# Round 0's second outputs before round 1's transposes, and a closing slot of round 1 without conversions begun: a fused RWKV-6 and MLP kernel

## The chip, the cores and the metric

The kernel runs on one core of a Trainium2 chip. The metric is the device time of one execution in microseconds, the median of several runs. Before the change it is 594.73 us (four runs: 592.81, 593.84, 595.62, 599.49). The run of 595.62 us is the one that was profiled; its span is 593.6 us.

The engines are named as in the profile: PE (TensorE matmul), PEld (its weight load), DVE (VectorE), ACT (ScalarE), POOL (GpSimd), SP (SyncE, which issues most of the DMAs here). Each engine takes its instructions in order, and an instruction that waits holds up all those behind it on its engine.

## The reference

Two stages in float32. The first is a linear attention with a state per head (batch 4, 8 heads, 768 steps, head dimension 48):

```python
for t in range(S):
    kt, vt, rt, wt = (k[:, :, t], v[:, :, t], r[:, :, t], w[:, :, t])
    cur = np.einsum('bhd,bhe->bhde', u[None] * kt, vt)
    y[:, :, t] = np.einsum('bhd,bhde->bhe', rt, state + cur)
    state = wt[:, :, :, None] * state + np.einsum('bhd,bhe->bhde', kt, vt)
```

Its output, as 4 x 768 x 384, goes through a normalised MLP with a residual:

```python
mu = np.mean(x, axis=-1, keepdims=True)
var = np.mean((x - mu) ** 2, axis=-1, keepdims=True)
xn = (x - mu) / np.sqrt(var + 1e-06) * g_ln
ch = np.maximum(xn @ w_ch1, 0.0) @ w_ch2
return (x + ch).astype(np.float32)
```

## The kernel before

The work is cut into eight rounds (four batches by two halves of 384 steps), and each round into two units of four heads. Units are numbered on: round 0 has units 0 and 1 (`u0`, `u1`), round 1 has 2 and 3 (`new[0]`, `new[1]` in the opening), and so on.

For a unit, `turned` transposes w, k and r with PE into PSUM (`w_ps`, `k_ps`, `r_ps`) and ACT copies the result to SBUF (`wT`, `rkT`). The part of the output that comes from inside a chunk of 64 steps is built in six levels: `quads` makes small matmuls into `a_ps`, `grow` multiplies r and k by products of decays on DVE, and `keep` moves the masked result from `a_ps` into `A`. `totals` makes the products of decays (`tot`, `decay`) for a round. At the end of a round `ends` transposes k (`kn_ps`, copied by ACT to `kn`), `finish` copies what is left of A and r, `states` multiplies k and v into `kv` and walks the state over the chunks on DVE (`s`), `exchanged` copies half of it across partitions on ACT (`sx`). `own_outputs` and `outputs` put the result together in PSUM (`y`), and DVE adds the term of u (`vo`, from `own_term` on POOL) to give `x`. That term needs `product_sums`, which multiplies the products r times k (`ruk`, from `products`) by u on PE, and a copy by ACT to `own`.

Then the MLP of the round: `moments` (statistics on DVE), `norm` (a root on ACT, `rstd`, then a reciprocal and three scalings on DVE, `xn`), `turned_x` (PE into `xT_ps`, ACT to `xT`), and `mlp`, a generator. One step of it is three matmuls and, in its first half, the ReLU on ACT: twelve steps make `h` from `h_ps`, and the later ones make `o_ps`. The matmuls of the MLP fill PE between the small stages of the attention part. They use two PSUM buffers in turn (`ps_m`), so a step needs the ReLU of two steps before it. Transposes use two others (`ps_t`), and `a_ps`, `kv` and `y` two more (`ps_a`).

The MLP weights are 24 parts of 128 x 384. They come in as raw words and are converted once, in rounds 0 and 1. For a part, `begin` makes three activations on ACT (a `w_sb` and two of `held` or `rest`) and issues the fetch of the part four further on; `join` is `shifted` (two DVE instructions) and `added` (one). From part 12 on, the rest goes into four buffers in turn, so `begin` of a part needs the join of the part four before it. A part must be joined before the MLP step that reads it.

The order on each engine is that of the program text for everything recorded through the wrapped engines (`PE`, `ACT`, `DVE`, `POOL`, `SPO`); loads through the plain `SP` are placed by the scheduler. The opening (lines 697 to 776) writes the order out by hand. From round 1 on the slots (round, level) are filled by `fill`, which spreads a list of tasks over the MLP steps that the slot gets (`UNTIL`); `mixed` interleaves lists by their relative place. In round 1 each slot adds begins and joins by two tables:

```python
JOINS, BEGINS = (3, 3, 3, 4, 4, 4), (3, 3, 3, 3, 4, 2)
```

The last slot of round 1 (level 5) is called the closing slot here. `warm` issues matmuls on zeros (`idle` in the profile); three columns of 128 make one matmul, two rows in the profile.

Of the kernel before, what the change touches and what calls it, by code (L numbers as in the profile page):

```python
# [52 lines left out]
def kernel(  # L53
# [31 lines left out]
    NLEV = 6  # L85
# [181 lines left out]
    def join():  # L267
        shifted()
        added()
# [89 lines left out]
    def product_sums(q):  # L359
        b, f, g = units[q]  # L360
        a = st[q]
        ps = ps_t.tile([P, RN], F32, tag="t", name=f"own_ps{q}")
        for pr in pairs:
            for c in range(TT):
                PE.matmul(
                    ps[:, ts(pr * TT + c, 2)], a["ruk"][pr][:, ts(c, P)],
                    sel[:, NP * g + pr], start=True, stop=True,
                )
        o = a["own"] = p4.tile([P, TT, NH], F32, tag="own", name=f"own{q}")
        ACT.copy(  # L370
            out=o.rearrange("p c (r j) -> p r c j", j=2),
            in_=ps[:, 0 : 2 * NK].rearrange("p (r c j) -> p r c j", r=NP, j=2),
        )

    def own_term(q, eng):
        a = st[q]
        a["vo"] = p4.tile([P, TT, NH, D], F32, tag="vo", name=f"vo{q}")
        eng.tensor_tensor(
            out=a["vo"], in0=vn[q],
            in1=a["own"][:, :, :, None].broadcast_to([P, TT, NH, D]), op=ALU.mult,  # L380
        )
# [117 lines left out]
    def exchanged(q):  # L499

        a = st[q]
        a["sx"] = p2.tile([P, NP, TT, D], F32, tag="sx", name=f"sx{q}")
        for j in range(2):
            ACT.copy(
                out=a["sx"][ds(HP * (1 - j), HP)],
                in_=a["s"].rearrange("p r (c i) e -> p r c i e", i=2)[ds(HP * j, HP), :, :, 0],
            )
# [3 lines left out]
    def own_outputs(q, tag="a"):  # L511

        y = ys[q] = banks(tag, f"y{q}")
        A = a_bufs[q // U % 2]
        for k_ in range(NK):
            pr, c = divmod(k_, TT)
            for i in range(2):
                for j in range(2):
                    rows = ds(C * (i ^ j), C)
                    PE.matmul(  # L520
                        y[j][ds(C * i, C), k_], A[rows, j, q % U, k_, :],
                        vx[q][rows, c, pr] if j else vn[q][rows, c, 2 * pr],
                        start=k_ == 0, stop=False, skip_group_check=True,
                    )
# [157 lines left out]
    def run(tasks):  # L682
        for t in tasks:
            t()

    def units_of(rnd):
        return [U * rnd + g for g in range(U)] if rnd < NR else []
# [37 lines left out]
    ahead = each(turned, new[:1], "wrk", pairs) + each(turned, new[1:], "wrk", pairs)  # L725
# [22 lines left out]
    exchanged(u0)  # L748
    states(u1)
    product_sums(u1)  # L750
    own_term(u1, POOL)
    own_outputs(u0)
    warm(3, "t")
    outputs(u0)
    exchanged(u1)
    own_outputs(u1, "m")
    warm(3, "t")
    run(ahead[8:])
    quads(new[0], 0)
    join()  # L760
    outputs(u1)
    load(units_of(2)[0], "w", SPO)
    load(units_of(2)[1], "w", SPO)
    products(new[1], POOL)
    begin()
    moments(0)
    shifted()
    quads(new[1], 0)
    product_sums(new[0])
    warm(6)  # L770
    norm(0)
    added()
    begin()
    join()
    run(each(turned_x, [0], range(KC)))
    mlps.append(mlp(0))

# [5 lines left out]
    while len(UNTIL) < NR * NLEV:  # L783
        UNTIL.append(UNTIL[-1] + MLP_STEPS // NLEV)
    ahead = [t for nm in "wkr" for t in each(turned, units_of(2), nm, pairs)]
    JOINS, BEGINS = (3, 3, 3, 4, 4, 4), (3, 3, 3, 3, 4, 2)
    for rnd in range(1, NR + 1):
        old, now, new = units_of(rnd - 1), units_of(rnd), units_of(rnd + 1)
        if rnd == 1:
            old = []  # L790
        for lev in range(NLEV):
            slot = (rnd - 1) * NLEV + lev
            if rnd == 2:

                for q in old if lev < 2 else []:
                    (states, outputs)[lev](q)
                if lev < 2:
                    mlp_step()
            elif old and lev < 2 * U:
                (states if lev < U else outputs)(old[lev % U])  # L800
            for q in now:
                if slot:
                    quads(q, lev)
            for which in ("rk",) if lev < NLEV - 1 else "kr":
                for q in now:
                    grow(q, lev, which)
            if now:
                if rnd == 1 and lev == 0:
                    totals(rnd, DVE)
                keep(rnd, lev)  # L810
            tasks = []
            if rnd == 1:
                if lev < 2:
                    tasks += each(load, new, "kr"[lev], [SPO])
                if lev == 2:
                    SPO.dma_start(
                        out=u_bc,
                        in_=bass.AP(
                            tensor=u.tensor, offset=u.offset, ap=[[0, P], [D, H], [1, D]]
                        ),  # L820
                    )
                    tasks += each(load_v, now, [SPO])
                if lev == 3:
                    tasks += each(load_vx, now, [SPO])
                if lev == 1:
                    tasks += each(product_sums, now[1:])
                if lev in (4, 5):
                    own_term(now[lev - 4], POOL)
            if rnd == 2 and lev == 0:
                tasks += each(load_v, now) + each(load, new, "w")  # L830
            if rnd == 2 and lev == 2:
                for q in now:
                    take(DVE, q)
                    tasks += each(load, new[q % U :][:1], "kr")
            if rnd == 2 and lev in (3, 4):
                tasks += each(own_term, now[lev - 3 :][:1], [POOL])
            if rnd > 2 and lev < 2:
                tasks += each(load, new, ["w", "kr"][lev])
            first = 3 if rnd == 2 else 1
            if rnd > 1 and new and first <= lev < first + 3:  # L840
                m = lev - first
                tasks += each(turned, new[m - 1 : m], "kr", pairs) if m else each(
                    turned, new, "w", pairs
                )
            if rnd == 2:
                if lev == 0:
                    tasks += each(exchanged, old)
                if lev == 1:
                    tasks += [lambda: moments(1), lambda: norm(1)]
                if lev == 2:  # L850
                    tasks += each(turned_x, [1], range(KC))
            elif old and lev < U:
                tasks += each(exchanged, [old[lev]])
            if lev == 3 and rnd > 1:
                for q in now:
                    load_vx(q)
                for q in new:
                    load_v(q)
                if rnd > 2:
                    moments(rnd - 1)  # L860
                    tasks += each(norm, [rnd - 1])
            if lev == 4 and rnd > 2:
                tasks += each(turned_x, [rnd - 1], range(KC))
                tasks += each(own_products, new[:1], [POOL])
            if lev == NLEV - 1:

                if now:
                    mlp_step()
                if rnd > 2 and new:
                    own_sums(new[0])  # L870
                if rnd == 2:
                    tasks += each(own_products, new[:1], [POOL]) + each(own_sums, new[:1])
                if rnd >= 2:
                    tasks += each(own_term, new[:1], [POOL])
                    tasks += each(own_products, new[1:], [POOL])
                    tasks += each(own_sums, new[1:]) + each(own_term, new[1:], [POOL])
                if new:
                    tasks += each(totals, [rnd + 1], [POOL])
                if now:
                    tasks = mixed(  # L880
                        tasks,
                        each(ends, now, pairs) + each(finish, [2, 2, 4])
                    )
            if rnd == 1:

                n = (1, 2, 2, 1, 0, 0)[lev] * NP
                tasks += mixed([begin] * BEGINS[lev], [join] * JOINS[lev], ahead[:n])
                del ahead[:n]
            fill(UNTIL[slot], tasks)
            if lev == (2 if rnd == 2 else 4) and old:  # L890
                mlps.append(mlp(rnd - 1))
# [32 lines left out]
```

## Time and profile before

| | |
|---|---|
| median of four runs | 594.73 us |
| profiled run | 595.62 us, span 593.6 us |
| PE busy | 571.2 us, 96% |
| PEld busy | 383.3 us, 65% |
| DVE busy | 279.1 us, 47% |
| ACT busy | 195.4 us, 33% |
| POOL busy | 93.8 us, 16% |
| mean granted PE clock | 0.989 |

The busy shares are means over stages that differ. The span in 40 slices of 14.8 us (a digit is a tenth; PEclk is the granted clock in tenths of full speed) shows where they differ:

```profile
PE   8999998799999999899999999999999999999997
DVE  4877998668365444425255334426245431130000
ACT  3557786303352125211243114321241015301200
PEclk9989999799999999989999999999999999999999
```

Slices 0 to 2 hold the load and round 0. In slices 4 and 5 (59 to 89 us) DVE and ACT are as busy as PE, with the conversion of the weights beside round 1. Slice 7 (104 to 119 us) is the end of round 1 and the start of round 2. From there on DVE and ACT have slack, and PE is busy nearly throughout.

### The profile page before, as it was taken

The page shows a single profiled execution, that of the slowest core. Times are in us where ns is not written, and L with a number is a line of the kernel's source. Part 1 is how long each engine was busy: PE and PEld are TensorE (multiplying, and loading weights), DVE is VectorE, ACT ScalarE, POOL GpSimd, SP SyncE. Part 2 cuts the span into 40 slices and gives each one's busy share as a digit, 9 for nine tenths or more (in the row PEclk, how much of TensorE's full clock was granted, in tenths as well). Part 3 has the DMA queues.
Part 4 walks back from the last instruction along what each step waited for, and adds up shares of the span by engine and source line. Part 5 has one row for each costly group of instructions (what it writes and reads, how often), then busy time and mean ns, then how long its engine had stood idle before and what let it go on. Part 6 is the DMA issues. An engine that isn't in the chain of part 4 may idle for free.

```text
span 593.6 us, 19016 instructions
## 1 busy us (share of the span) xinstructions
PE 571.2 (96%) x8540; PEld 383.3 (65%) x8540; DVE 279.1 (47%) x574; ACT 195.4 (33%) x426; POOL 93.8 (16%) x118
## 2 busy tenths in 40 slices
PE   8999998799999999899999999999999999999997
PEld 5776765466666666666666666667666665666554
DVE  4877998668365444425255334426245431130000
ACT  3557786303352125211243114321241015301200
POOL 6041022004260026000250006100240000000000
PEclk9989999799999999989999999999999999999999
DMA  9974995046323402331013402012000000000000
GB/s 145 207 188 116 230 215 123 1 89 119 58 44 65 105 15 41 59 73 40 24 34 62 93 17 55 2 32 59 15 2 3 15 28 2 1 15 27 0 14 27
DMA packets 120528, 36.52 MB, mean 62 GB/s; under 512 B 114176, under 2 KB 117376, under 8 KB 120448
## 3 DMA queue, kind: packets, MB, share of 16 engines
q1 hardware_dynamic: 118048, 35.01, 27.2%
q8 instruction: 67, 1.10, 0.8%
q10 hardware_dynamic: 2400, 0.30, 0.6%
q14 instruction: 13, 0.11, 0.1%
HBM read 28.51 MB, written 4.72 MB: 56 GB/s over the span
## 4 chain that ended last, share of the span: by engine, by line
PE 90%; ACT 3%; DVE 3%; issue 2%; POOL 1%; DVEq 0%; ACTq 0%; POOLq 0%
PE o_ps L49 31%; PE h_ps L49 31%; PE a_ps L49 12%; PE y L49 4%; PE k_ps L49 2%; PE kv L49 2%; PE w_ps L49 2%; PE r_ps L49 2%; PE kn_ps L49 2%; PE xT_ps L49 1%; PE idle L49 1%; ACT rest L49 1%; DVE rkT L49 1%; POOL mask L49 1%; PE own_ps L49 1%
## 5 line engine op out<-in xcount | busy, mean ns | idle before, releaser
L49 PE MATMUL o_ps<-w_sb,h 128*128 128x384 f32 x576 | 200.9, 495 | 1.4 <-ACT h L49 1.4
L49 PE MATMUL h_ps<-xT,w_sb 128*128 128x384 f32 x576 | 197.2, 490 | 0.0
L49 PEld LDWEIGHTS o_ps<-w_sb,h 128*128 128x128 f32 x576 | 106.1, 193 | 64.2 <-issue 2.7
L49 PEld LDWEIGHTS h_ps<-xT,w_sb 128*128 128x128 f32 x576 | 105.0, 190 | 62.3
L49 ACT ACTIVATE h<-h_ps 128x384 f32<-128x384 f32 x96 | 46.9, 489 | 141.3 <-PE h_ps L49 141.0
L49 PEld LDWEIGHTS a_ps<-rkT 48*64 48x64 f32 x4608 | 75.0, 136 | 25.6 <-issue 19.5
L49 PE MATMUL a_ps<-rkT 48*64 48x32 f32 x4608 | 80.3, 221 | 10.0 <-issue 5.6
L49 DVE TENSOR_TENSOR rkT<-rkT,tot 128x768 f32<-128x768 f32 (+1 forms) x96 | 78.9, 860 | 19.1 <-PE a_ps L49 10.7
L49 DVE TENSOR_TENSOR o<-o_ps,x 128x384 f32<-128x384 f32 x24 | 13.4, 557 | 135.2 <-PE o_ps L49 135.1
L49 POOL TENSOR_TENSOR vo<-v,own 128x576 f32<-128x576 f32 x16 | 19.7, 1233 | 294.3 <-DVE own L49 263.8
L49 DVE COPY_PREDICATED A<-mask,a_ps 128x768 f32<-128x768 int8 x40 | 53.3, 1333 | 0.0
L49 DVE SCALAR_TENSOR_TENSOR s<-s,decay,kv 128x48 f32<-128x48 f32 x160 | 29.3, 258 | 32.1 <-PE kv L49 32.1
L49 DVE TENSOR_TENSOR x<-y,vo 128x288 f32<-128x288 f32 x32 | 13.1, 452 | 60.1 <-PE y L49 60.1
L49 ACT ACTIVATE xT<-xT_ps,g_sb 128x384 f32<-128x384 f32 x24 | 13.6, 580 | 58.2 <-PE xT_ps L49 58.2
L49 ACT COPY rkT<-k_ps 128x384 f32<-128x384 f32 x32 | 14.4, 478 | 51.1 <-PE k_ps L49 51.1
L49 ACT COPY rkT<-r_ps 128x384 f32<-128x384 f32 x32 | 14.7, 478 | 33.1 <-PE r_ps L49 33.1
L49 DVE TENSOR_SCALAR w_sb<-w_sb 128x384 f32<-128x384 f32 (+1 forms) x48 | 18.6, 388 | 3.6 <-ACT w_sb L49 2.7
L49 ACT ACTIVATE rstd<-mv,eps 128x3 f32<-128x3 f32 x8 | 2.4, 296 | 50.3 <-DVE mv L49 50.2
L49 DVE TENSOR_REDUCE own<-rk 128x12 f32<-128x576 f32 x12 | 9.0, 750 | 20.6 <-POOL rk L49 20.6
L49 ACT COPY wT<-w_ps 128x384 f32<-128x384 f32 x32 | 14.3, 479 | 13.0 <-PE w_ps L49 8.0
L49 DVE TENSOR_TENSOR rkT<-rkT,wT 128x768 f32<-128x768 f32 x16 | 17.9, 1149 | 0.5 <-PE a_ps L49 0.3
L49 PEld LDWEIGHTS y<-v,A 64*64 64x64 f32 x384 | 13.3, 139 | 7.1 <-issue 6.0
(71 smaller groups left out, 515.6 us busy)
## 6 DMA issues: line engine op xcount, KB each, us to landing
raw<-in_moe_w_ch_dram SPq DMA_DIRECT2D x24, 384.0 KB, 4.1
nat_w<-in_w_dram SPq DMA_DIRECT2D x48, 96.0 KB, 2.9
nat_k<-in_k_dram SPq DMA_DIRECT2D x48, 96.0 KB, 3.0
v<-in_v_dram SPq DMA_DIRECT2D x48, 96.0 KB, 3.7
out_dram<-o SPq DMA_DIRECT2D x24, 192.0 KB, 1.9
nat_r<-in_r_dram SPq DMA_DIRECT2D x45, 96.0 KB, 3.0
vx<-v SPq DMA_DIRECT2D x28, 72.0 KB, 2.6
nat_r<-in_r_dram ACTq DMA_DIRECT2D x3, 96.0 KB, 4.0
```

The source lines that it names most:

```text
L49: return lambda *args, **kw: self.tc.keep_in_program_order(f(*args, **kw))
```

## The change

The opening is put into another order, and the tables of begins and joins are changed, with the closing slot built in its own way.

- `outputs(u1)` follows `own_outputs(u1)` at once; `moments(0)` follows it. The transposes of k and r of unit 3 (`ahead[8:]`) and both `quads` come after.
- One `join` stands before `outputs(u0)`; a `begin` and the next `shifted` stand behind `exchanged(u1)`, and a second `begin` behind `moments(0)`. `added` follows on `moments` on DVE, ahead of the norm.
- The loads of w for round 2 come behind these begins, so behind their fetches on SP.
- `products(new[1])` moves from POOL, where it stood ahead of the norm, to DVE behind the norm and the third join.
- The idle matmuls: `warm(3, "t")` between the outputs and the transposes goes, and `warm(6)` becomes a `warm(3)` on each side of `product_sums(new[0])`. One matmul less in all.
- In round 1 the begins per slot are 3, 3, 4, 4, 3 and the joins 3, 4, 4, 4, 4, 2. The closing slot begins nothing; its two joins stand first in the list of tasks and `totals` last. The opening holds three begins behind round 0's levels, one more than the two it had apart from those in the levels; the sum is 24 as before.

On PE (apart from that matmul) and ACT the instructions only change places; POOL loses one multiplication of 128 x 768 and DVE gains it.

```diff
     product_sums(u1)
+    join()
     own_term(u1, POOL)
     own_outputs(u0)
     warm(3, "t")
     outputs(u0)
     exchanged(u1)
+    begin()
+    shifted()
     own_outputs(u1, "m")
-    warm(3, "t")
-    run(ahead[8:])
-    quads(new[0], 0)
-    join()
     outputs(u1)
+    moments(0)
+    begin()
     load(units_of(2)[0], "w", SPO)
     load(units_of(2)[1], "w", SPO)
-    products(new[1], POOL)
-    begin()
-    moments(0)
-    shifted()
+    run(ahead[8:])
+    added()
+    quads(new[0], 0)
     quads(new[1], 0)
+    warm(3)
     product_sums(new[0])
-    warm(6)
+    warm(3)
     norm(0)
-    added()
     begin()
     join()
+    products(new[1])
     run(each(turned_x, [0], range(KC)))
     mlps.append(mlp(0))
...
-    JOINS, BEGINS = (3, 3, 3, 4, 4, 4), (3, 3, 3, 3, 4, 2)
+    JOINS, BEGINS = (3, 4, 4, 4, 4, 2), (3, 3, 4, 4, 3)
...
-                if new:
-                    tasks += each(totals, [rnd + 1], [POOL])
+                    if new:
+                        tasks += each(totals, [rnd + 1], [POOL])
                 if now:
                     tasks = mixed(
                         tasks,
                         each(ends, now, pairs) + each(finish, [2, 2, 4])
                     )
-            if rnd == 1:
+                if rnd == 1:
+                    tasks = [join] * JOINS[lev] + tasks + each(totals, [rnd + 1], [POOL])
+            if rnd == 1 and lev < NLEV - 1:
 
                 n = (1, 2, 2, 1, 0, 0)[lev] * NP
                 tasks += mixed([begin] * BEGINS[lev], [join] * JOINS[lev], ahead[:n])
```

## The prediction

> **What bounds the kernel now.** I read the page first: PE is busy 96% of the span and the chain that ended last is 90% PE, so only time in which PE stands still or runs slowly can be won. Next came the PE waits:
>
> ```profile
> PE a_ps L49 <- issue: 5.6, 5, 1.9
> PE a_ps L49 <- DVE s L49: 4.4, 1, 4.4
> PE o_ps L49 <- ACT h L49: 1.4, 1, 1.4
> ```
>
> One wait stands out: 4.4 us, once. The PE timeline places it at the end of round 1 (columns: start, us, engine, instruction; in brackets the idle time before):
>
> ```profile
> 103.87 2.20 PE L49 MATMUL o_ps<-w_sb,h 128*128 128x384 f32 x6
> 110.49 2.79 PE L49 MATMUL a_ps<-rkT 48*64 48x32 f32 x96 [4.42 <-DVE s L49]
> 113.21 6.09 PE L49 MATMUL o_ps<-w_sb,h 128*128 128x384 f32 x12
> ```
>
> The matmuls behind the gap are slow too: this a_ps takes 2.79 us where the next one, at 125.74, takes 1.60. The stretches by window say why (after the stretch and its length: busy us and count of PE, PEld, DVE, ACT and POOL; then the granted PE clock, the DMA share and GB/s):
>
> ```profile
> 106.00:110.50 4.50, 0.08 (x2) 0.04 (x2) 3.83 (x17) 2.09 (x5) 0.00 (x0) 0.98 0.00 0
> 110.50:116.40 5.90, 5.90 (x101) 4.49 (x102) 5.24 (x13) 1.60 (x4) 0.00 (x0) 0.50 0.01 3
> 116.40:119.30 2.90, 2.90 (x12) 1.36 (x12) 0.00 (x0) 0.00 (x0) 0.00 (x0) 0.86 0.00 0
> ```
>
> The gap costs 4.42 us plus 5.9 x 0.50 + 2.9 x 0.14 = 3.4 us of clock: 7.8 us. DVE's timeline shows what s waited for:
>
> ```profile
> 96.11 1.96 DVE L49 TENSOR_TENSOR rkT<-rkT,tot 128x384 f32<-128x384 f32 x4
> 97.98 1.91 DVE L49 TENSOR_SCALAR w_sb<-w_sb 128x384 f32<-128x384 f32 x2
> ...
> 105.43 0.76 DVE L49 TENSOR_SCALAR w_sb<-w_sb 128x384 f32<-128x384 f32 x2 [2.73 <-ACT w_sb L49]
> ...
> 108.52 3.58 DVE L49 SCALAR_TENSOR_TENSOR s<-s,decay,kv 128x48 f32<-128x48 f32 x20
> ```
>
> Four joins stand between the last grow and s, and the last two wait for two begins that ACT reaches only after its kn, A and rx copies. Between 53 and 98 us DVE never rests, so a join taken out of this slot has to go where DVE is full.
>
> **Part one: the closing slot.** Two begins (1.57 us each, from 68.71 to the next row at 70.28) and two joins (1.37 us each: three fill 67.29 to 71.41) leave it; the 2.73 us wait goes with them. The two joins that remain took 97.98 to 102.6, so 4.6 us instead of 2.74: POOL's totals run from 98.21 to 102.8 beside them. Totals go last in program order, but POOL has nothing else there and starts them when DVE's last grow is read, as now: no change.
>
> **Part two: where the work goes.** On DVE, one join more in slot 1, one more in slot 2 (3,3,3,4,4 becomes 3,4,4,4,4), and the product ruk of unit 3, which was POOL's (1.84 us); the nearest DVE row, tot<-wT of the same 128x768, is 0.95. With the start of the stage 0.35 earlier (part three) and 0.24 of idle time used, the last grow ends 0.95 + 2 x 1.37 - 0.35 - 0.24 = 3.1 later at most; step by step I get 100.7 instead of 97.98. Two joins at 4.6 bring DVE to s at 105.3 and s of the first unit (10 of the 20 rows, 1.8) to 107.1.
>
> On ACT, begins become 3,3,4,4,3: one more in slot 2, one more in slot 3. In slot 1 the first is also recorded after h instead of before it, when ACT was idle until 65.65. ACT then runs without a pause from 65.4: h, begin, wT, begin, h, k, begin, k, h, begin, k, begin, h, k. Five begins at 1.57 and nine short ones at 0.36 end that at 76.5, and the last k copy of the second unit is at its end. Now it is here:
>
> ```profile
> 74.53 0.45 ACT L49 COPY rkT<-k_ps 128x384 f32<-128x384 f32 x1
> ...
> 74.62 0.97 PE L49 MATMUL r_ps<-ident,nat_r 128*128 128x128 f32 x6
> ```
>
> The second r_ps needs the buffer that this copy empties. PE arrives at 74.6 and goes on at 76.55: a new wait of 1.95 us. From begin 16 on, each begin also waits for the join four back. DVE joins 12 and 13 end at 79.6 and 82.6 (POOL's two vo, 2.98 us, stretch DVE by 1.6, as they stretched the grow at 78.42 from 1.82 to 3.42), then grow and keep until 85.3, joins 14 to 17 until 90.75. ACT follows: begin 18 ends at 87.75, begin 19 at 89.3, and only then comes h of step 9, so PE's step 11 waits from 88.5 to 89.75; begins 20 and 21 put the last h at 93.9, where o_ps needs its buffer, another 1.5. In place of the 1.39 of now PE loses 4.7, and it reaches kn at 100.9 instead of 98.41, and the end of its fill at 108.6 instead of 106.07. What kn needs, the first k of the last grow, is there at 99.4, so DVE alone would allow 99.4.
>
> What is late next: s is done at 107.1, PE free at 108.6. The gap is gone, and it is PE that comes last. a_ps starts 110.49 - 108.6 = 1.9 earlier and runs at full clock, which gives 3.3 more (1.2 at a_ps, 2.79 for 1.60, and 2.1 at the twelve o_ps, 6.09 for about 4.0). **Sum of the closing slot: 5.2 earlier.** Bounds: at least 0 for the 1.9 if ACT is later than I walked it, at most 110.49 - 107.1 = 3.4 if ACT delays nothing, with the 3.3 in either case unless a new pause lets the clock fall.
>
> **Part three: the opening.** y of the second unit is finished before the transposes: on PE it takes the place of an idle pair (0.84) with its own 0.75, so r_ps starts as now. x is ready at 45.2 instead of 48.5 and moments at 46.9 instead of 50.27. Yet the norm hardly gains, for ACT's queue is in order and rstd stands behind the copy of own:
>
> ```profile
> 49.78 0.17 ACT L49 COPY own<-own_ps 128x12 f32<-128x12 f32 x1 [1.45 <-PE own_ps L49]
> 50.31 0.30 ACT L49 ACTIVATE rstd<-mv,eps 128x3 f32<-128x3 f32 x1 [0.36 <-DVE mv L49]
> ```
>
> own_ps has the same PE work in front of it (a_ps twice, and an idle pair moved there), so own comes at about 49.95 and rstd at 50.15. The other 0.2 is the shift that stood between rstd and the reciprocal on DVE. 0.35 us is what I count, with 0 to 0.7 as bounds. It is inside the 3.1 and the walk above, not added again. The moved join lies in DVE's idle 2.13 us before x; the two begins lie in ACT's idle 3.36 us before r_ps; one idle pair less costs nothing while PE waits for xn. On SP the two raw loads now go ahead of the six nat_w of round 2 and wait for these begins, until 44.4 instead of being issued from 33.86; six issues took 7.1 us and landing 4.3 at the median, so the first unit's arrive near 52 and the second's near 56, against w_ps at 55.67 and 63.18. nat_k stays behind the next raw, at 52.6. No cost; if the first came after 55.3, it would delay PE one to one.
>
> One low stretch is a risk. From 38.84 to 42.05 the granted clock is 0.50 although PE shows as busy, after 7.5 us of narrow matmuls without an idle pair (31.4 to 38.8). The change makes the stretch behind 41.7 pair-free until 47.6, 5.9 us; before it was 5.5 (44.1 to 49.6) and kept 1.00. I take 0, with 3.4 x 0.5 = 1.7 as the upper bound.
>
> The Trainium skill (TensorE: Matmul & The Clock Gate, section "Why this matters for your kernels") says that only pauses over about 3 us halve the clock. The 4.42 us row agrees; the row at 38.84 does not, since there was no pause. By the page alone the opening's risk would be 0 and the new waits of 1 to 2 us would cost themselves alone.
>
> **The numbers.** The profiled execution took 595.62 with a span of 593.6; 593.6 - 5.2 = 588.4, with the 2.0 around it 590.4. Its time is 0.9 over the median of 594.73, so 589.6 on the median: 0.9% faster, just inside the 1% that I take as the least this kernel's measurement can tell from no change.
>
> **Rivals.**
> - A: ACT delays less than walked, and DVE alone sets the pace: 3.4 + 3.3 = 6.7, so 588.0. For it: a begin whose join is done does not wait, and each of my ACT waits rests on a difference of a microsecond. Against: ACT is busy 4.49 of 5 us from 90 to 95 already. Chance 0.27.
> - B: the clock falls in the opening: 5.2 - 1.7 = 3.5, so 591.2. Chance 0.14.
> - C: the gap only shrinks: DVE is later than 105.3 (the moved joins meet POOL) and a pause of 2 us is left, or the change does not empty the slot in effect; 2 to 3 us won: 592.2. Chance 0.11.
> - D, slower: the waits of PE for h at 88.5 and at 92 grow beyond a pause that the clock survives. 1.39 kept 1.00, 4.42 did not; from about 3.4 on the lost clock comes back, 3.4 us in the new place, and the longer wait itself puts a_ps at or behind 110.5: 5.2 - 3.4 - 2.5 = 0.7 slower, 595.4, and with a second such pause 3.4 more, 598.8. Against: two of my walked waits would have to double. Chance 0.10.
> - My forecast, 588.5 to 591: 0.38.
>
> Range 586.9 to 595: it leaves out the upper part of D and the tail of A. Faster by over 1% (under 588.8) is most of A and an edge of the forecast, 0.31; slower by over 1% (over 600.7) is D with more than one such pause, 0.05; the rest, 0.64.
>
> **What would show it.** In the new profile PE's wait for s is under 1 us and the clock beside the first a_ps of round 2 is 1.00; if a gap above 3 us is there, the main step is wrong. r_ps waits for ACT's rkT by about 2 us near 75, and h_ps and o_ps wait for ACT's h by about 2.7 together near 88 to 94; without these, A holds. rstd follows own within 0.3 us, and moments end 3 us before it; if rstd starts near 47, the opening gains up to 3 us more and I misread ACT's queue. A clock of 0.50 between 42 and 52 is B. Shifts of the time after 120 us that differ from the shift at the first y of round 2 would make the account wrong.

## The result, and the profile after

The changed kernel took 593.17 us (median of 43 runs, 588.74 to 602.17), the kernel before 596.21 us in the runs beside it (64 runs, 592.38 to 604.1). The ratio is 0.9952, with an interval of 0.9935 to 0.997: 0.5% faster, about 2.9 us, where 5.2 us or 0.9% had been forecast. The profiled execution took 594.14 us with a span of 592.2.

The gap at the end of round 1 is gone. In the waits of PE in the new kernel (what waited, for what: us in total, times, longest) no row names s any more; these are those that the text comes back to:

```profile
PE a_ps L49 <- issue: 6.0, 6, 1.8
PE r_ps L49 <- ACT rkT L49: 1.9, 2, 1.7
PE k_ps L49 <- ACT rkT L49: 1.5, 2, 1.2
...
PE o_ps L49 <- ACT h L49: 1.0, 1, 1.0
```

In PE's timeline the first a_ps of round 2 follows its predecessor without a pause and takes 1.60 us:

```profile
93.75 3.49 PE L49 MATMUL o_ps<-w_sb,h 128*128 128x384 f32 x10 [0.97 <-ACT h L49]
100.74 0.82 PE L49 MATMUL kn_ps<-ident,rkT 128*128 128x128 f32 x6
106.19 2.20 PE L49 MATMUL o_ps<-w_sb,h 128*128 128x384 f32 x6
108.33 1.60 PE L49 MATMUL a_ps<-rkT 48*64 48x32 f32 x96
109.86 4.14 PE L49 MATMUL o_ps<-w_sb,h 128*128 128x384 f32 x12
```

The same stretches by window that the prediction showed (columns as there) have PE busy throughout at a clock of 1.00. Two stretches further back in the same execution run at 0.50 all the same, with no pause of PE inside them:

```profile
106.00:110.50 4.50, 4.50 (x124) 3.17 (x117) 4.42 (x21) 2.77 (x7) 0.00 (x0) 1.00 0.01 4
110.50:116.40 5.90, 5.90 (x179) 4.19 (x180) 3.12 (x4) 0.00 (x0) 0.00 (x0) 1.00 0.06 12
247.00:250.20 3.20, 3.20 (x8) 1.99 (x7) 1.66 (x2) 0.48 (x1) 0.00 (x0) 0.50 0.25 51
455.00:458.40 3.40, 3.40 (x6) 1.84 (x6) 1.77 (x2) 0.00 (x0) 0.00 (x0) 0.50 0.02 5
```

DVE reaches s with two joins in front of it and hardly waits:

```profile
98.44 1.96 DVE L49 TENSOR_TENSOR rkT<-rkT,tot 128x384 f32<-128x384 f32 x4
100.32 1.91 DVE L49 TENSOR_SCALAR w_sb<-w_sb 128x384 f32<-128x384 f32 x2
105.63 3.59 DVE L49 SCALAR_TENSOR_TENSOR s<-s,decay,kv 128x48 f32<-128x48 f32 x20 [0.60 <-PE kv L49]
```

Where the time went was read by measuring from marks, since the start of an execution varies by some us with its loads. From the first x of round 0 on DVE to the first y of round 2 on PE the kernel before takes 76.39, 76.20, 76.35, 76.06 and 75.47 us in five profiles (77.92 in a sixth, with two more half-clock stretches inside), the new one 71.13, 71.48 and 71.17. So the touched stretch became 4.8 us shorter between the means of the five and the three, near the 5.2 forecast, and 2.9 arrived. About 2 us are given back outside it.

They are in two things. The first is a new pause of PE. In the rounds behind, this a_ps of the kernel before runs through:

```profile
334.43 1.58 PE L49 MATMUL a_ps<-rkT 48*64 48x32 f32 x92
335.94 0.88 PE L49 MATMUL k_ps<-ident,nat_k 128*128 128x128 f32 x6
```

In the new kernel the same instructions are broken after 58 of the 92, by a pause in which PE waited for nothing that the profile shows ("issue"):

```profile
329.95 1.11 PE L49 MATMUL a_ps<-rkT 48*64 48x32 f32 x58
332.13 0.77 PE L49 MATMUL a_ps<-rkT 48*64 48x32 f32 x34 [1.07 <-issue]
332.83 0.87 PE L49 MATMUL k_ps<-ident,nat_k 128*128 128x128 f32 x6
```

The pause stands there in all three profiles of the new kernel (1.07, 0.96, 1.22) and in none of six of the kernel before. From the first y of round 2 to the end, the two profiles of the kernel before that have no half-clock stretch there take 471.06 and 471.07 us; the one such profile of the new kernel takes 472.37. The second thing is the clock: the half-clock stretches behind the gap are gone, but on the mean of all executions their count fell by 1.2, not by the two that the gap had brought.

### The profile page after: what moved, and what is told of

Read it like the earlier page. It is cut to its first block, busy times and chain, and to the rows that moved or that the text cites. A ratio compares the mean times of both kernels' runs of the same rounds, so it can differ in the third digit from the quotient of the medians.

```text
span 592.2 us, 19009 instructions
## 1 busy us (share of the span) xinstructions
PE 572.5 (97%) x8538; PEld 384.3 (65%) x8538; DVE 280.0 (47%) x575; ACT 195.2 (33%) x426; POOL 88.6 (15%) x117
## 4 chain that ended last, share of the span: by engine, by line
PE 89%; ACT 4%; DVE 3%; issue 2%; POOL 1%; DVEq 0%; ACTq 0%; POOLq 0%
PE o_ps L49 32%; PE h_ps L49 30%; PE a_ps L49 11%; PE y L49 4%; PE kv L49 2%; PE k_ps L49 2%; PE w_ps L49 2%; PE r_ps L49 2%; PE kn_ps L49 2%; PE xT_ps L49 1%; ACT rest L49 1%; PE idle L49 1%; DVE w_sb L49 1%; ACT w_sb L49 1%; POOL mask L49 1%
## 5 line engine op out<-in xcount | busy, mean ns | idle before, releaser
L49 PEld LDWEIGHTS h_ps<-xT,w_sb 128*128 128x128 f32 x576 | 105.6, 191 | 62.8 <-issue 0.6
L49 PEld LDWEIGHTS a_ps<-rkT 48*64 48x64 f32 x4608 | 73.8, 135 | 21.6 <-issue 14.0
L49 PE MATMUL a_ps<-rkT 48*64 48x32 f32 x4608 | 79.0, 219 | 6.0 <-issue 6.0
L49 PEld LDWEIGHTS r_ps<-ident,nat_r 128*128 128x128 f32 x96 | 12.3, 149 | 9.4 <-issue 3.6
L49 PE MATMUL r_ps<-ident,nat_r 128*128 128x128 f32 x96 | 16.0, 289 | 2.3 <-ACT rkT L49 1.9
```

Of the source, the lines that this page charges most:

```text
L49: return lambda *args, **kw: self.tc.keep_in_program_order(f(*args, **kw))
```

## The experiments

Each ratio is against the kernel before on the same chip, in the same runs, with its 95% interval. "Before" and "after" in a heading name the kernel that the edit starts from.

**Both kernels again.** The kernel before, unchanged:

> The kernel before once more, for the granted clock of each of its executions. The profile of before lost 4 windows of 3.4 us at half clock in all, two of them after the 4.4 us gap; the changed kernel's 44 executions lost between 0 and 8, about 3 at the median (a mean clock of 0.991). Theory 1 (the gap always costs its two windows, as profiled): about 2 windows more than the changed kernel on average, so a mean clock near 0.985 and no execution without a low window. Theory 2 (two windows in the profile were an unlucky place of the gap; often it costs one or none): at most 1 window more, a mean clock of 0.988 to 0.991, and the difference of 5.2 us that the two profiles show at the first y of round 2 is more than the kernels differ on average. Ratio to before 1.000.

596.4 us, ratio 1.000 [0.997, 1.003]. Its profile has the gap of 4.41 us and two half-clock stretches behind it, from 111.0 to 117.9. The kernel after, unchanged, twice:

> The changed kernel once more, beside the closing slot alone on the same chip. Theory 1 (the new opening loses 1 to 2 us, by low clock windows or otherwise): 0.3 to 0.6% faster than before, and 1 to 2 us behind the closing slot alone. Theory 2 (the openings are equal, as predicted to 0.35 us, and the difference of the first comparison was chance): 0.6 to 0.8% faster, within 1 us of the closing slot alone.

> The changed kernel a third time, for its mean number of low clock windows beside that of before on the same chip (3.1 against 4.3 so far; the gap of before alone always costs 2). If the two windows of the gap were the whole clock difference: 2 fewer. If the changed kernel has about 0.8 more elsewhere, as so far: 1.2 fewer, and 0.4 to 0.6% faster.

591.04 us, 0.9937 [0.9911, 0.9963], and 593.63 us, 0.9927 [0.9892, 0.9962]. The first of these profiles has no half-clock stretch at all and a span of 586.9; the last has five and a span of 593.4. The same instructions, 6.5 us apart, so single executions of this kernel can't be compared without counting those stretches.

**The closing slot alone.** The opening of before, with the new tables and the new closing slot:

```diff
-    JOINS, BEGINS = (3, 3, 3, 4, 4, 4), (3, 3, 3, 3, 4, 2)
+    JOINS, BEGINS = (3, 4, 4, 4, 4, 2), (3, 3, 4, 4, 4)
```

(the closing slot as in the change; BEGINS ends on 4 because the opening holds one begin less)

> Only the closing slot and the tables are changed (the begin that the opening does not hold is given to slot 4: 3,3,4,4,4); the opening is that of before. Prediction's account: nearly the whole gain, since the opening was worth 0.35: 0.5 to 0.9% faster, the gap before the first a_ps of round 2 gone. Rival (the opening is what gains, or the removed idle pair loses what the slot wins): under 0.3%, or over 0.9%. The DVE product ruk is back on POOL, so the last grow ends about 0.6 earlier than in the changed kernel.

> The closing slot alone, again. Theory 1: 0.7 to 0.9% faster than before and ahead of the changed kernel by 1 to 2 us. Theory 2: equal to the changed kernel within 1 us.

591.86 us, 0.9926 [0.9893, 0.9959], and again 593.63 us, 0.9974 [0.9947, 1.0001]. PE does not wait for s in either profile; its last o_ps waits 2.30 and 2.16 us for ACT's h. The two runs of one kernel lie 0.5% apart, as much as the effect; pooled they equal the whole change.

**The opening alone.** The new opening in the kernel before, with the closing slot and the tables of before, apart from one begin:

```diff
-    JOINS, BEGINS = (3, 3, 3, 4, 4, 4), (3, 3, 3, 3, 4, 2)
+    JOINS, BEGINS = (3, 3, 3, 4, 4, 4), (3, 3, 3, 3, 4, 1)
```

(the opening as in the change; BEGINS ends on 1 because the opening holds one begin more)

> Only the opening is changed; the closing slot keeps four joins and has one begin. Prediction's account: 0.35 us earlier at the first h_ps and the gap of 4.4 us still there, perhaps shorter by the 1.57 us of one begin: 0 to 0.4% faster. Rival (the low stretch without an idle pair lets the clock fall in the opening): 0.2 to 0.5% slower, with a low window between 42 and 56 us.

597.88 us, 1.002 [0.998, 1.006]: the opening by itself gains nothing. PE's timeline still has a gap ahead of the first a_ps, shorter than before's by 1.56 us, about what a begin takes (1.57), and the a_ps is as slow as behind the long one:

```profile
114.37 2.79 PE L49 MATMUL a_ps<-rkT 48*64 48x32 f32 x96 [2.86 <-DVE s L49]
```

The row of the stretch around it (start to end, length, busy us of PE, PEld, DVE, ACT, POOL, then the clock) shows half clock for 6.8 us with a pause of 2.86, from 0.8 us before the pause ends:

```profile
113.60:120.40 6.80, 6.03 (x101) 4.53 (x102) 6.02 (x17) 1.72 (x4) 0.00 (x0) 0.50 0.01 2
```

**The gap filled with idle matmuls.** The kernel before, with PE kept at work while it waits for s:

```diff
                 if lev < 2:
                     mlp_step()
+                if lev == 0:
+                    warm(12, "t")
```

> The kernel before with four idle matmuls of 128x384 (3.3 us) put into the gap of the closing slot, ahead of the first a_ps of round 2; nothing else moves and the gap stays as long. It prices the clock alone. Theory 1 (the gap always costs two windows): 3.3 us or 0.55% faster, clock 1.00 beside a_ps. Theory 2 (it costs one window or none on average): 0.1 to 0.3% faster. If PE were held back by the idle matmuls, slower.

593.8 us, 0.9957 [0.9925, 0.9989]. The one profile is of the slowest of its twelve executions (600.16 us). In it a_ps still waits for s, but runs at full clock:

```profile
112.31 2.76 PE L49 MATMUL idle<-nought 128*128 128x384 f32 x8
116.80 1.60 PE L49 MATMUL a_ps<-rkT 48*64 48x32 f32 x96 [1.73 <-DVE s L49]
```

A stretch of half clock follows all the same, from 118.77 to 122.19, just behind this a_ps. The ratio prices the clock that the filling repairs: 2.6 us, between 0.7 and 4.5. No work was won here, and yet the time is about that of the whole change.

**Is it always two stretches?** The kernel before, one profile each:

> The kernel before, one more profile, to see what the gap of the closing slot costs in each execution. Theory 1 (the gap always costs two low windows and 3.3 us): from the first x of round 0 to the first y of round 2 it takes 76.2 to 76.4 us as in the two profiles so far, with half clock for 6.8 us from the end of the gap. Theory 2 (where the windows fall decides, 1.25 on average): in one or more of four profiles only one low window follows, or the low clock begins inside the gap, and the stretch is 1 to 2 us shorter.

> As the look before: 76.2 to 76.4 us and 6.8 us of half clock by theory 1, 74.5 to 75.5 us by theory 2 in some of the four.

> As the look before: 76.2 to 76.4 us and 6.8 us of half clock by theory 1, 74.5 to 75.5 us by theory 2 in some of the four.

> As the look before: 76.2 to 76.4 us and 6.8 us of half clock by theory 1, 74.5 to 75.5 us by theory 2 in some of the four.

596.34, 591.1, 593.59 and 595.88 us. Each has the gap and 6.8 us of half clock at its end: 114.67 to 121.5, 109.22 to 116.04, 108.52 to 115.34, 111.58 to 118.4. With the two earlier profiles of this kernel and that of the opening alone it is seven of seven. 6.8 us are two units of 3.41, the length that the single stretches elsewhere have too. Theory 1 is right in the count. Of its 76.2 to 76.4 us only the first look keeps within the bounds (76.35); the second has 76.06, the fourth 77.92 with its two stretches further ahead. In the third the low clock begins 1.64 us before the gap ends, and that is the shortest, 75.47: as Theory 2 had it, where the two units fall matters, by up to 0.9 us.

**One idle matmul back.** The kernel after, with the one matmul that the change took out put back ahead of the transposes:

```diff
     load(units_of(2)[1], "w", SPO)
+    warm(3, "t")
     run(ahead[8:])
```

> The changed kernel with the removed idle pair (0.84 us) put back ahead of the transposes of unit 3, where PE waits 1.2 us for ACT's copy of r in the changed profile. If the low stretch without an idle pair is what loses in the new opening: fewer low windows than the changed kernel (about 0.4 less) and 0.5 to 1 us faster than it. If not: equal to it within 0.5 us.

591.46 us, 0.9933 [0.9906, 0.9961], not to be told from after's 591.04 beside it. Read only for the opening this says that the idle matmul is harmless there. The pause near 330, however, is not in its profile, and that is taken up below.

**The norm ahead of own.** In the kernel after ACT's rstd is ready to run when the moments end, and stands in ACT's queue behind the copy of own, which waits for PE:

```profile
49.99 0.17 ACT L49 COPY own<-own_ps 128x12 f32<-128x12 f32 x1 [3.13 <-PE own_ps L49]
50.05 0.30 ACT L49 ACTIVATE rstd<-mv,eps 128x3 f32<-128x3 f32 x1
```

DVE's rows are the other side of it; the moments end at 46.74 and the reciprocal waits 3.21 us:

```profile
46.44 0.30 DVE L49 BATCH_NORM_AGGREGATE mv<-stats 128x2 f32<-128x6 f32 x3
50.39 0.18 DVE L49 RECIPROCAL rstd<-rstd 128x3 f32<-128x3 f32 x1 [3.21 <-ACT rstd L49]
```

The edit puts the sums that feed own behind the norm:

```diff
     load(units_of(2)[1], "w", SPO)
+    warm(3, "t")
     run(ahead[8:])
     added()
     quads(new[0], 0)
     quads(new[1], 0)
-    warm(3)
-    product_sums(new[0])
-    warm(3)
     norm(0)
     begin()
     join()
+    product_sums(new[0])
     products(new[1])
```

> The changed kernel with the product sums of unit 2 (own_ps on PE, own on ACT) behind the norm and the begin, and without the two idle matmuls beside them; one idle pair ahead of the transposes. It tests the point that rstd waits behind own in ACT's queue. Expected: rstd near 47.2 instead of 50.05, first xT near 49.5 instead of 51.2, first h_ps about 1.7 us earlier, and since DVE starts slot 0 earlier too, about as much at the last grow: 1 to 2 us faster than the changed kernel. Rival: fewer idle matmuls let the clock fall more often in the opening, which takes 1 us or more back, or DVE's joins do not come earlier since begins are late: no gain.

> The norm-first kernel again, as the base of the next two. Its profile had the first h_ps at 50.67 (3.0 us before the changed kernel's 53.65) and the first a_ps of round 2 at 105.35 (3.6 before). If that gain is kept to the end: 0.9 to 1.2% faster than before, 2.5 to 4 us ahead of the changed kernel. If the first result was luck in the number of low clock windows: 0.6 to 0.8%.

588.01 us, 0.9902 [0.987, 0.9934], and 588.1 us, 0.9847 [0.9813, 0.988]. ACT now runs rstd first, and PE's transposes of x and its first h_ps start 2.1 and 2.9 us earlier (51.23 and 53.61 in the kernel after):

```profile
46.82 0.30 ACT L49 ACTIVATE rstd<-mv,eps 128x3 f32<-128x3 f32 x1
49.26 0.17 ACT L49 COPY own<-own_ps 128x12 f32<-128x12 f32 x1 [0.58 <-PE own_ps L49]
```

```profile
49.09 0.95 PE L49 MATMUL xT_ps<-ident,xn 128*128 128x128 f32 x6
50.67 2.10 PE L49 MATMUL h_ps<-xT,w_sb 128*128 128x384 f32 x6
```

From the first x to the first y of round 2 it takes 68.1 us, 3.2 less than after, where 1 to 2 had been expected. This version is faster than both kernels.

**What sets the pace in round 1.** Two edits of the norm-first kernel. The first begins one conversion earlier, so that ACT's k copy, which r_ps waits for, comes sooner:

```diff
-    JOINS, BEGINS = (3, 4, 4, 4, 4, 2), (3, 3, 4, 4, 3)
+    JOINS, BEGINS = (3, 4, 4, 4, 4, 2), (4, 3, 3, 4, 3)
```

> The norm-first kernel with one begin moved from slot 2 to slot 0 (4,3,3,4,3), where ACT is idle for 2.4 us. It tests the prediction's wait of r_ps for ACT (1.7 us in the changed kernel's profile) and which engine sets the pace of slots 1 to 4. If ACT does: the wait goes and kn and the first a_ps of round 2 come 1 to 1.7 us earlier, 0.2 to 0.3% faster than the norm-first kernel. If DVE does (continuous from 53 to 105 us): the wait goes but comes back as another wait further on, and a_ps moves by less than 0.4 us.

591.15 us, 0.9899 [0.9854, 0.9945]. The wait of r_ps falls to 0.2 us, and an h_ps at 86.91 waits 1.29 for ACT's h in its place. Counted from the first x, a_ps of round 2 starts after 63.98 us, against 62.50 and 62.46 in the norm-first kernel: no gain. Ahead of it this profile holds two half-clock stretches, at 49.9 and 87.4, and those of the norm-first kernel hold none there, so how much of the new wait is the edit's own is not settled. The second gives the product ruk of unit 3 back to POOL:

```diff
+    products(new[1], POOL)
     norm(0)
     begin()
     join()
     product_sums(new[0])
-    products(new[1])
```

> The norm-first kernel with the product ruk of unit 3 back on POOL, ahead of the norm. If DVE sets the pace of slots 1 to 4: the last grow, kn and the first a_ps of round 2 come 0.6 to 0.95 us earlier. If ACT sets it: no change. If POOL's product beside the norm slows DVE (as vo slowed the grow by 1.6): the norm is later by up to 1 us and the gain is gone.

588.64 us, 0.9853 [0.9815, 0.9891]. DVE, freed of 0.95 us, waits 0.93 us for PE's a_ps at 69.88 instead, and beside POOL's product its three scalings of the norm take 2.55 us, 1.26 without it. Counted from the first x, the last grow starts after 53.93 us, against 52.63 and 52.58: no gain either, with one half-clock stretch in the way, from 50.20 to 53.62. That PE, ACT and DVE set the pace of round 1 in turn, each close behind the next, fits both profiles; it is not shown by them.

**The pause near 330.** Listing every "issue" pause of PE over 0.6 us shows that, beyond the opening, they stand at the same instructions in every profile of one kernel, and move by a few instructions with the length of PE's program ahead of them. The pause near 250 leaves 35 of its 96 a_ps in the kernel before, 34 in the closing slot alone and with the idle matmul back, 33 in the opening alone, 32 after, 30 or 31 in the norm-first kernels. Those with 32 or fewer have the pause near 330; those with 33 or more don't. Counted in PE's rows of the trace from the start of the program, the places are the same in every kernel: 4292 or 4293 rows stand ahead of the pause near 250 in all twenty profiles, and 5566 to 5568 ahead of the one near 330 wherever there is one. What moves is the a_ps that falls there. So two kernels moved PE's program by four instructions and left everything else: an idle matmul counts as two, and the eight idle blocks of 128 columns at the start of the program are three matmuls. The norm-first kernel with the same eight blocks as five matmuls:

```diff
-    warm(8)
+    for n in (2, 2, 2, 1, 1):
+        warm(n)
```

> The norm-first kernel with the eight idle columns at the start of PE issued as five matmuls (2, 2, 2, 1, 1) in place of three (3, 3, 2): the same columns, four instructions more ahead of everything else on PE. Theory P (the extra PE pause of about 1.1 us in an a_ps near 326, with 'issue' beside it, depends on where that a_ps lies in PE's program, counted in instructions): the a_ps group behind the pause near 243 shrinks or grows with the shift, from x30 to x34, and the pause near 326 is gone; the time falls by about 1.1 us against the norm-first kernel, to 586.9 and a ratio near 0.984 by the pooled 0.988, less 0.002. Theory Q (the pause comes from what the changed stage leaves behind, transfers or the earlier time, and not from the place in the program): the pause near 326 stays at 1.0 to 1.2 us, and the time stays at 588. Neither theory expects a change at the start beyond 0.3 us.

The kernel before with three blocks, one matmul, at the start (the texts on record call the blocks columns):

```diff
-    warm(8)
+    warm(3)
```

> The kernel of before with three idle columns at the start of PE in place of eight: four instructions fewer ahead of everything else, and all else as before. Theory P: the a_ps group behind the pause near 252 goes from x35 to about x31, and a pause of about 1.1 us that no profile of before has appears in an a_ps near 330 to 336; at an equal number of low-clock windows the time rises by 1.1 us, 0.2 per cent. Theory Q: no such pause, and the time stays within 0.1 per cent. The gap of 4.4 us ahead of the first a_ps of round 2, with two windows of half clock behind it, stays under both.

The lengthened norm-first kernel (587.79 us, 0.9876 [0.9838, 0.9913]) has lost the pause; this a_ps runs through:

```profile
325.24 1.58 PE L49 MATMUL a_ps<-rkT 48*64 48x32 f32 x92
```

The shortened kernel before (599.94 us, 1.0061 [1.003, 1.0093]) has gained it, at the very same instruction as after:

```profile
337.33 1.11 PE L49 MATMUL a_ps<-rkT 48*64 48x32 f32 x58
339.38 0.71 PE L49 MATMUL a_ps<-rkT 48*64 48x32 f32 x34 [0.95 <-issue]
```

Theory P holds in both directions for the pause: it belongs to the place of that a_ps in PE's program, not to what the changed stage does. The counts near 250 came out as expected too, 34 and 31. The 1.1 us that the lengthened kernel was to gain are not clear of the noise: 0.9876 lies in the intervals of both norm-first runs. On the start both theories missed: with five idle blocks fewer PE waits for its first loads, and a pause near 27 us grew to 3.12, with 6.83 us of half clock behind it, so the 0.6% of that kernel is not the price of the pause alone.

**All executions together.** Half-clock stretches of 3.41 us occur by chance in every kernel here. Their number in an execution follows from its clock: (1 - clock) x span x 2 / 3.41. A straight line through all 290 timed executions, with one height for each kernel and one slope for all, gives 1.48 us for one such stretch, and for each kernel the time at no stretch (the interval is 95%; for a kernel all of whose executions have some, it is extrapolated: the kernel before never has fewer than two, the opening alone and the shortened kernel never fewer than three):

| kernel | executions | mean us | stretches, mean | us at no stretch |
|---|---|---|---|---|
| before | 115 | 595.9 | 4.3 | 589.6 ± 0.4 |
| opening alone | 12 | 597.7 | 5.0 | 590.4 ± 0.7 |
| gap filled | 12 | 594.3 | 3.1 | 589.8 ± 0.7 |
| closing slot alone | 24 | 592.7 | 3.2 | 588.0 ± 0.5 |
| after | 67 | 593.2 | 3.1 | 588.7 ± 0.4 |
| after, one idle matmul back | 12 | 591.1 | 2.4 | 587.6 ± 0.7 |
| norm first | 18 | 588.6 | 2.4 | 585.0 ± 0.5 |
| norm first, begins early | 6 | 591.2 | 4.4 | 584.7 ± 1.0 |
| norm first, product on POOL | 6 | 588.5 | 2.0 | 585.6 ± 0.9 |
| norm first, program longer | 6 | 587.9 | 2.6 | 584.1 ± 0.9 |
| before, program shorter | 12 | 599.4 | 5.4 | 591.4 ± 0.8 |

The rows price the pause: after is 1.1 ± 0.7 above the same kernel with its idle matmul back, and the norm-first kernel 0.95 ± 1.0 above its longer form; the profiles give 0.96 to 1.22. Only the first of the two is clear of zero, and narrowly: with a height for each chip it is 0.8 ± 0.8, and on one chip the means of the two kernels are 591.2 and 591.1. That the pause comes and goes is shown; its price rests mostly on its length in the profiles. The other pauses of issue vary by as much from one execution to the next. Taken off, they leave the same work: from the first y of round 2 to the end, less all pauses of issue over 0.6 us, it is 466.0 to 466.5 us in the five profiles without a half-clock stretch there, with the pause near 330 (two) or without it. The rows also price the gap's wait without its clock: 1.6 ± 0.5 (closing slot alone) and 2.0 ± 0.7 (idle matmul back) below before. And filling the gap does not move the last column measurably, and moves the count by 1.25, which is what a repair of the clock alone should do, though short of the two stretches of the gap.

## Why the prediction was right and where it was wrong

**The gap and its clock, right.** PE comes last and there is no wait for s. a_ps of round 2 starts at 108.33, 108.90 and 108.65 in three profiles (forecast 108.6), at full clock. DVE gets to its two joins at 100.3 (the last grow was to end at 100.7) and to s at 105.6 (105.3); kn is at 100.74 (100.9). Counted from the first x, kn comes some 2.6 us later than before and a_ps 4.5 sooner after kn: the moved joins cost what was walked, and the emptied slot gave it back with more. Rivals C and D are out. For A, the first y would have had to come 1.5 us sooner than it does; B's half clock between 42 and 52 is not there but for its first microsecond in one of the three profiles, where a stretch from 39.55 ends at 42.96; another has one right behind, from 52.25 to 55.66.

**ACT's new waits, right in kind.** r_ps waits 1.70 us (forecast 1.95), the last o_ps 0.97 (1.5). The wait of h_ps, 1.25 in the forecast, is nothing in two profiles and 0.9 in one. So PE waited 2.7 us in the first profile and 3.5 in the second, where 4.7 had been walked. That kn came on time in the first is partly luck: its chance stretch from 52.25 to 55.66 takes the place of some of the waits that stayed away. Not forecast was a wait of k_ps for ACT's r copy in the opening, 1.2 and 1.5 us in two profiles: the two begins moved there, taken to lie in idle time, hold ACT until 44.9. On PE own_ps follows k_ps without a further wait, and rstd stands behind own, so this wait lies ahead of the norm; what it costs was not tested by itself.

**The opening, right in its order, and in its number partly by luck.** own at 49.99 against 49.95, rstd at 50.05 against 50.15, moments 3.3 us before it. Two misses cancel in this: r_ps starts at 43.33, 0.77 sooner than the forecast that it "starts as now", and k_ps then waits the 1.2 us for ACT. The norm-first kernel shows that it was ACT's queue: with own taken out of the way the same moments gain 3.2 us.

**"One idle pair less costs nothing while PE waits for xn": this step failed.** This is the term that the prediction put at nothing. In the opening nothing speaks against it: with the matmul back it takes 71.65 us from the first x to the first y of round 2, against 71.1 to 71.5. 280 us later it is not true: PE's program is two rows shorter (8540 to 8538), and an a_ps that used to run through stops for 1.1 us. With the idle matmul back the pause is gone. It is not the idle matmul alone: the opening alone has the same 8538 rows and leaves 33 near 250, without the pause; the new closing slot moves the place by one more (34 left, where before has 35), and only both together reach 32. That the place in the program decides was shown by making the pause in the kernel before and by removing it from the norm-first kernel, each time by the length of the program alone. The prediction listed the symptom, a shift behind 120 us that differs from that at the first y of round 2, as what would make its account wrong; the profile before had the hint in its first wait row, a_ps <- issue, five times, up to 1.9, which the prediction shows and does not ask after.

**"Runs at full clock, which gives 3.3 more": the term was too large.** The mechanism is right, seven profiles of seven, and the shortened kernel's is an eighth (113.37 to 120.19). But the count of half-clock stretches fell by 1.2 on the mean, not by 2, and one stretch is worth 1.48 us on the mean of all executions, not 1.65: 1.8 us instead of 3.3. The gap's own two stretches cost the 3.3 in the profile before, less where they begin inside the gap; what was not in the sum is that others come by chance, in the profiles after near 245 to 270 and 455 above all, and that the new kernel has more of those (0.8 ± 0.5 an execution, if the gap always has its two). Whether the change brings them, or an execution that has not just been at half clock is more likely to fall there, stays open: the other kernels without the gap have 2.0 to 4.4. The gap-filled kernel, which moves no work, has 3.1 like the new one; but its profile shows a stretch right behind the 1.73 us that PE still waits. From chip to chip the mean of the new kernel itself goes from 1.8 to 3.4.

Together: 5.2 forecast, less 1.1 for the pause, less 1.5 for the clock, makes 2.6, against 2.7 between the two means of the table and 2.9 by the ratio. The rest is inside the intervals.

The rule that was weighed there, from the Trainium skill (TensorE: Matmul & The Clock Gate, section "Why this matters for your kernels"), is to leave no pause of PE over about 3 us, since an idle window brings back the half clock. The 4.42 us of before fit it, and so do the 2.86 us of the opening alone, which brought as much half clock. What the rule does not lead one to expect are stretches at 0.50 behind pauses of only 0.93 us: those at 246.8 and 455.0 above follow pauses of issue that end at 246.09 and 454.58.

## What to carry to other kernels

An edit that adds or drops even one "free" matmul in PE's long unrolled program moves all that stands behind it, and here a short pause of issue 280 us further on appeared or vanished with it; where a gain of the touched stretch doesn't reach the end, compare those pauses between the profiles before asking for a new theory. An engine's queue in program order is part of the critical path: a copy of 0.17 us that waits for another engine, put ahead of a ready step, held that step up for 3.2 us here. And where a chance event of 1.5 us happens several times an execution, count it in each run, and compare kernels at an equal count.

## What the runs showed of the hardware that was not expected

- The half clock comes in units of 3.41 us: one or more by chance, two (6.8 us) at the gap in eight profiles of eight. Within one execution the starts lie whole multiples of 3.41 apart (7.88, 52.25, 246.81, 263.88 and 455.02 in the new kernel's profile: 13, 57, 5 and 56 units). The number in one execution ranged from 0 to 10 over all kernels. Between the two sizes of pause, one of 2.29 us in the opening alone has a stretch 1.35 us behind its end, and those of 2.30 and 2.16 in the closing slot alone have none. The late chance ones begin within 1.6 us of the end of a pause of issue of 0.7 to 1.9 us in a run of narrow a_ps (246.09 and 246.8, 262.40 and 263.9, 454.58 and 455.0 in the new kernel's profile). The same pauses stand in its second profile, where the clock is 1.00 throughout, so they do not suffice; what decides was not tested.
- Pauses of issue of 0.7 to 1.9 us stand at fixed instructions of PE's program. A shift by two to four instructions made one of about 1 us appear or go, behind the 62nd to 64th of 96 a_ps, while the four others behind 150 us only moved along by three or four. Behind the opening the places are 2125, 3272, 4292, 4547 and 7478 rows from the start in the kernel before, 5566 besides in its shortened form; the steps between them (1147, 1020, 255, 1019, 1912) are 9, 8, 2, 8 and 15 times 127.5, to within a row. So the pauses seem to go with a fixed length of PE's program. Why only some of those places pause was not found.
